# A table of steps for a router and eight experts: one small product one chunk later, one group behind another, two widenings moved into the last round

## The chip, the cores and the metric

The kernel runs on one core of one Trainium2 chip. The time is that of the device for one execution, in microseconds (us). The engines are TensorE (PE, with PEld for its loads of weights), VectorE (DVE), ScalarE (ACT), GpSimd (POOL) and SyncE (SP, which issues most DMAs). Each runs its own instructions in order and waits on semaphores for the others. TensorE has two clocks, 1.2 and 2.4 GHz; the profile tells the one granted as a share of the higher (0.50 or 1.00).

## The reference

```
x   = causal softmax attention(q, k, v)          # 2 x 12 heads x 448 x 64, gathered to 896 x 768
logits = x @ w_gate                              # 896 x 8
# greedy: in the order of falling logit, a token takes an expert that has fewer than 112 tokens
for e in range(8):
    h = maximum(x[assigned == e] @ w1[e], 0)     # 112 x 768 @ 768 x 1024
    y[assigned == e] = h @ w2[e]                 # 112 x 1024 @ 1024 x 768
yn  = y / sqrt(mean(y * y, -1) + 1e-6) * rms_g
out = (silu(yn @ w_g) * (yn @ w_val)) @ w_out    # 768 -> 1536 -> 768, all 896 rows
```

Everything is in 32-bit floats. Where a product is split, each operand is the sum of a rounded high part (hi) and the rest (lo), and three products stand for one: hi by hi, lo by hi, hi by lo.

## The kernel before

Attention comes first, head by head, then eight rounds, one for an expert each, then the rest of the feed-forward part. The rounds are written as strings of words, which a function emits one after the other; TensorE, VectorE, ScalarE and GpSimd carry out their instructions exactly in that written order, whereas SyncE's loads and the feed-forward part behind the rounds are put in order by a scheduler. Round 0 uses the string ITER0, rounds 1 to 5 ITER, round 6 ITER6 and round 7, which has no next expert, LASTR; END follows. A word is a letter, a chunk number, and an optional `'` or `+` for work that belongs to another round.

- `U0` to `U7`: eight chunks of the expert's first product (hp, line 626, six matmuls each, on the gathered and transposed rows xf and the raw weights). `A`, `H`: its relu (ScalarE, hh, line 634) and the low part of that (VectorE, hl, line 638).
- `Z0` to `Z7`: a chunk of the second weights is split, hi by a cast on ScalarE (line 574), lo on VectorE (line 575). `Z0+` belongs to the next round. `D0` to `D7`: the second product (y, line 651, six matmuls each).
- `N0` to `N2`: the norm of the previous expert's y (lines 660 to 666, result yn). `Y0`, `Y1`: its transposes (tp, line 587) and the split of them (xnh on ScalarE, xnl on VectorE, lines 598 and 599).
- `X0`, `X1`: transposes of the next expert's gathered rows (tp<-cs,xg) and the copies xf of them on ScalarE (line 596).
- The router of a later round: `M1` transposes the best logits m to rows mr (line 402) and copies them to ms on ScalarE; `G` (lines 411 to 415) compares, `P0` to `P6` count (pc, line 423), `Q0`, `Q1` rank and pick an expert, `O` makes a one-hot tile (VectorE, line 493), `F0'` multiplies it with token numbers (pi, line 501, seven small matmuls), `F1'` makes row numbers idx of that (VectorE, line 505) and issues the gather xg, `Q2'` names the expert, whose weights may then be loaded.
- `B0` to `B7` load half-rows of the feed-forward weights (SyncE, w, line 519), `C0` to `C7` widen them (a cast g on ScalarE, line 524, then five operations on VectorE, lines 528 to 532, about 2.45 us in all), `J` splits the widened halves (lines 536, 537), `I0` and `I1` make the table of output rows (pr, line 690, its two copies to ms, line 692; pt, line 696, idt on VectorE, line 697), `K` are the first gate products (line 548).

PSUM tiles of the router (mr, pc, ptot, pi, pr, pt) share the tag "r", which has two banks. `M1` asks for two of them, one for four transposes and one for three:

```
for t0, t1 in ((0, 4), (4, NT)):
    mr = bank("r", "mr")
    for t in range(t0, t1):
        nc.tensor.transpose(mr[:, (t - t0) * 128:(t - t0 + 1) * 128],
                            self.m[:, t:t + 1].to_broadcast([128, 128]), ident)
    nc.scalar.copy(self.ms[:, t0 * 128:t1 * 128], mr[:, :(t1 - t0) * 128])
...
with tc.manual_schedule(engines={ET.PE, ET.Activation, ET.DVE, ET.Pool}):
    emit(START0, -2)
    emit(START1, -1)
    for r in range(E):
        emit(ITER0 if r == 0 else LASTR if r == E - 1 else ITER6 if r == E - 2 else ITER, r)
    emit(END, E)
```

Of the kernel before, what the change touches and what calls it, by code (L numbers as in the profile page):

```python
# [24 lines left out]
F1 = 1024  # L25
# [10 lines left out]
START0 = 'M0 M1 G G'  # L36
START1 = "G1' G' P0' P1' G' P2' P3' P4' G' P5' G1' P6' Q0' Q1' M1 O' G F0' F1' G P0 P1 Q2' G G G P2 P3 G X0 P4 P5 G X1 P6 U0+ Q0 U1+ U2+ Q1 U3+ U4+ O"
ITER0 = "Y1 A0 M1 N2 U5 G F0' G U6 Q2' F1' U7 Y0 G G G D0 N1 P0 P1 A1 P2 D1 D2 D3 G P3 D4 G X0 D5 P4 P5 P6 N0 D6 Q0 X1 D7 Z0+"
ITER = "U0 Q1' O' U1 Z1 Z2 N0 N1 U2 F0' F1' U3 Q2' A0 M1 N2 Z3 U4 H0 Z4 U5 Y0 Y1 Z5 G U6 G Z6 U7 A1 G D0 G P0 H1 G P1 D1 G D2 P2 Z7 G P3 D3 D4 D5 P4 P5 D6 X0 P6 D7 X1 Q0 Z0+"
LASTR = "U0 B2 U1 Z2 Z3 N0 N1 N2 I0 B3 U2 Z4 B4 U3 A0 B5 U4 Y0 Z5 H0 Y1 B6 U5 I1 Z6 C2 U6 B7 U7 A1 D0 H1 Z7 J0 D1 J1 C3 D2 D3 J2 C4 D4 J3 C5 D5 D6 D7 K0"  # L40
ITER6 = "U0 Q1' O' U1 Z1 Z2 N0 N1 U2 F0' F1' U3 Q2' A0 N2 Z3 U4 H0 Z4 U5 Y0 Y1 Z5 U6 Z6 U7 A1 D0 B0 H1 Z7 D1 B1 D2 D3 Z0+ D4 C0 D5 X0 Z1+ D6 C1 X1 D7"
PRE = 2
END = "N0 N1 N2 K1 Y0 Y1 J4 S0 J5 C6 K2 J6 C7 K3 J7 K4 K5 K6 S1 K7"
QK = 'dd'
# [27 lines left out]
def tile_attn_moe_ffn(ctx, tc, qk, v, consts, wts, wgv, wout, rmsg, out):  # L72
# [626 lines left out]
    def emit(words, r0):  # L699
        for w in words.split():  # L700
            op, c, r = w[0], int(w[1:].rstrip("'+") or 0), r0 + w.count("+")
            if op in "MGPQ" or op in "OF":
                k = r + 2 - (w[-1] == "'")
                if 0 <= k < E:
                    getattr(rounds[k], op)(c)
            elif op == "K":
                half, which, part = c // 4, c // 2 % 2, c % 2
                gate_val(half, which, range(3 * part, 3 * part + 3))
            elif op == "S":
                sg0[c] = cv.tile([128, S], F32, tag="sg", name="sg", bufs=2)  # L710
                nc.scalar.activation(sg0[c], gv0[c, 0][:, :S], AF.Silu)
            elif op == "Z":
                if r < E:
                    split(r, 8 + c)
            elif op == "I":
                turn_ids(c)
            elif op == "B":
                raws64.append(load64(half64(wgv, c)))
            elif op == "C":
                wide.append(widen(raws64[c]))  # L720
            elif op == "J":
                if c % 2 == 0:
                    early.append(tiles64())
                hi, lo = early[c // 2]
                c0 = c % 2 * 384
                halves(wide[c], hi[:, c0:c0 + 384], lo[:, c0:c0 + 384])
            elif op == "X":
                if r + 1 < E:
                    if c == 0 and r >= 0:
                        exps.append(Expert(r + 1))  # L730
                    getattr(exps[r + 1], op)(c)
            elif op in "NY":
                if r > 0:
                    getattr(exps[r - 1], op)(c)
            else:
                getattr(exps[r], op)(c)

    ET = mybir.EngineType
# [6 lines that stand above are left out]
# [143 lines left out]
```

## Time and profile before

| | us |
|---|---|
| three runs | 615.65, 613.38, 615.59 (median 615.59) |
| the profiled execution, its own time | 616.78 |
| its span in the profile | 615.0 |
| mean granted clock of TensorE | 0.972 |
| TensorE busy | 578.8 |
| VectorE busy | 468.1 |
| ScalarE busy | 271.6 |

A median is that of separate runs; the profile shows one more execution, of which all the rows below are. Its span goes from its first to its last instruction. A busy time sums what an engine works, without what it waits, so a time won is one in which TensorE stands still or runs at the lower clock.

### The profile page before, as it was taken

Reading aid. Unit: us, or ns where it says so; the run is one execution under the profiler, and the core shown is the slowest. Engines: PE = TensorE matmul, PEld = TensorE weight load, DVE = VectorE, ACT = ScalarE, POOL = GpSimd, SP = SyncE. Lnnn points to the kernel's source line nnn. Section 1 sums busy time; section 2 is a strip of 40 time slices with the busy share of each in tenths; the row PEclk is TensorE's granted clock in tenths of the full one; section 3 lists DMA queues with packets and bytes.
Section 4 is the critical chain, followed back from the end, with each engine's and each line's share of the span. In section 5 each row is a group of like instructions: output and inputs, shape, how many; then the busy total and the mean of one; then the engine's idle time right before and its main releaser. Section 6 shows DMA issues by size and latency. Waiting matters only on the chain.

```text
span 615.0 us, 11157 instructions
## 1 busy us (share of the span) xinstructions
PE 578.8 (94%) x3926; PEld 541.4 (88%) x3926; DVE 468.1 (76%) x1246; ACT 271.6 (44%) x617; POOL 97.6 (16%) x102
## 2 busy tenths in 40 slices
PE   4899999858999999999979999999999999999996
PEld 3799999748699999999969899999999999999995
DVE  7699999695588888978757799999998992991410
ACT  4799998501252353444434343444333434331200
POOL 4688775140100000000000000000000000000210
PEclk9999999957999999999979999999999999999998
DMA  8988881109996968869796243445444550000211
GB/s 276 259 253 256 244 242 41 31 6 376 317 355 227 335 219 309 284 210 350 279 345 194 78 138 122 151 155 144 125 141 130 155 134 21 27 1 1 103 39 39
DMA packets 47976, 109.35 MB, mean 178 GB/s; under 512 B 15232, under 2 KB 17408, under 8 KB 47920
## 3 DMA queue, kind: packets, MB, share of 16 engines
q1 hardware_dynamic: 45280, 93.96, 46.7%
q0 software_dynamic: 2640, 14.68, 7.5%
q8 instruction: 31, 0.51, 0.3%
q14 instruction: 25, 0.20, 0.1%
HBM read 103.12 MB, written 5.51 MB: 177 GB/s over the span
## 4 chain that ended last, share of the span: by engine, by line
PE 72%; DVE 13%; DMA 7%; issue 3%; ACT 2%; SPq 1%; POOL 1%; POOLq 0%; DVEq 0%; ACTq 0%
PE o L795 14%; PE pv L774 13%; PE pg L774 13%; PE hp L626 6%; PE sp L174 4%; PE pt L203 4%; PE ot L233 4%; PE y L651 4%; PE pn L260 3%; DMA raw<-in_wts 3%; DVE lo L575 2%; DVE G L415 2%; DMA w<-in_wgv 2%; PE pg L548 2%; DMA cs<-in_consts 2%
## 5 line engine op out<-in xcount | busy, mean ns | idle before, releaser
L626 PE MATMUL hp<-xf,raw 128*128 128x112 f32 x768 | 96.1, 284 | 4.0 <-ACT xf L596 4.0
L626 PEld LDWEIGHTS hp<-xf,raw 128*128 128x128 f32 x768 | 92.9, 200 | 4.9 <-ACT xf L596 4.4
L575 DVE TENSOR_TENSOR lo<-raw,hi 128x768 fp32r<-128x768 f32 x56 | 52.7, 955 | 15.3 <-ACT hi L574 15.0
L802 POOL DMA_INDIRECT out<-ob,idt x7 | 6.8, 969 | 306.9 <-ACT ob L801 298.4
L536 ACT CAST hi<-t 128x384 fp32r<-128x384 f32 x58 | 29.5, 510 | 49.2 <-DVE t L532 49.0
L195 ACT ACTIVATE pe<-sm,nm 128x256 f32<-128x256 f32 (+3 forms) x84 | 48.7, 582 | 2.5 <-DVE nm L185 2.1
L774 PE MATMUL pv<-xnh,hi 128*128 128x448 f32 x132 | 48.6, 368 | 0.0
L774 PE MATMUL pv<-xnl,hi 128*128 128x448 f32 x132 | 48.6, 368 | 0.0
L774 PE MATMUL pv<-xnh,lo 128*128 128x448 f32 x132 | 48.6, 368 | 0.0
L774 PE MATMUL pg<-xnh,hi 128*128 128x448 f32 x132 | 48.6, 368 | 0.0
L774 PE MATMUL pg<-xnl,hi 128*128 128x448 f32 x132 | 48.6, 368 | 0.0
L774 PE MATMUL pg<-xnh,lo 128*128 128x448 f32 x132 | 48.6, 368 | 0.0
L203 PE MATMUL pt<-cs,pe 128*128 128x128 f32 x228 | 41.3, 288 | 3.8 <-DVE ptl L220 2.6
L185 DVE CUSTOM_DVE_ANT_0 sm<-sp,mask 128x384 f32<-128x384 f32 (+3 forms) x84 | 42.1, 514 | 3.2 <-PE sp L174 2.3
L574 ACT CAST hi<-raw 128x768 fp32r<-128x768 f32 x56 | 44.3, 840 | 0.3 <-DMA raw<-in_wts 0.3
L524 ACT ACTIVATE g<-w 128x384 f32<-128x384 f32 x72 | 39.6, 553 | 8.8 <-DMA w<-in_wgv 8.7
L220 DVE TENSOR_TENSOR ptl<-pt,pth 128x512 fp32r<-128x512 f32 (+3 forms) x84 | 41.4, 514 | 2.5 <-ACT pth L216 2.5
L216 ACT CAST pth<-pt 128x512 fp32r<-128x512 f32 (+3 forms) x84 | 37.1, 444 | 10.9 <-PE pt L203 9.0
L529 DVE SCALAR_TENSOR_TENSOR t<-g,t 128x384 uint32<-128x384 uint32 x72 | 39.3, 554 | 0.2
L531 DVE SCALAR_TENSOR_TENSOR g<-w,g 128x384 f32<-128x384 uint32 x72 | 39.2, 554 | 0.2
L174 PE MATMUL sp<-hi 128*128 128x384 f32 (+3 forms) x84 | 32.9, 401 | 6.8 <-DVE hi L160 5.4
L532 DVE TENSOR_TENSOR t<-t,g 128x384 f32<-128x384 f32 x72 | 38.8, 554 | 0.2
(163 smaller groups left out, 1367.3 us busy)
## 6 DMA issues: line engine op xcount, KB each, us to landing
raw<-in_wts SPq DMA_DIRECT2D x128, 384.0 KB, 5.9
w<-in_wgv SPq DMA_DIRECT2D x48, 384.0 KB, 3.7
w<-in_wout SPq DMA_DIRECT2D x24, 384.0 KB, 3.1
hi<-in_qk POOLq DMA_DIRECT2D x10, 896.0 KB, 5.8
qr<-in_qk SPq DMA_DIRECT2D x11, 448.0 KB, 4.4
vr<-in_v SPq DMA_DIRECT2D x12, 224.0 KB, 3.0
xs<-xl SPq DMA_DIRECT2D x12, 224.0 KB, 3.2
kr<-in_qk SPq DMA_DIRECT2D x10, 224.0 KB, 3.3
```

What stands on the lines that cost most here:

```text
L174: nc.tensor.matmul(sp[:, :w], x[:, t * 128:t * 128 + 128], kh[:, w0:w0 + w], start=st, stop=not st)
L185: nc.vector.tensor_tensor_reduce(out=sm[:, :w], in0=sp[:, :w], in1=mask[:, MOFF[t]:MOFF[t] + w], op0=ALU.add, op1=ALU.min, scale=-0.125, s ...
L195: nc.scalar.activation(pe[:, :w], sm[:, :w], AF.Exp, bias=nm[:, t:t + 1], scale=-1.0, accum_out=sums[:, t:t + 1])
L203: nc.tensor.transpose(pt[:, b * 128:b * 128 + 128], pe[:, b * 128:b * 128 + 128], ident)
L220: nc.vector.tensor_sub(*rest.pop((h, t)))
L524: nc.scalar.activation(g, raw[:, :, 1].bitcast(F32), AF.Copy, scale=2.0 ** -112)
L529: nc.vector.scalar_tensor_tensor(t, gu, 0x80000000, t, op0=ALU.bitwise_and, op1=ALU.bitwise_or)
L574: nc.scalar.copy(hi, raw)
L575: nc.vector.tensor_sub(lo, raw, hi.bitcast(F32))
L626: nc.tensor.matmul(o, w[:, dc * 128:dc * 128 + 128], self.x[:, dc, :], start=(dc == 0), stop=(dc == 5))
L774: nc.tensor.matmul(dst[:, :S], w[:, dc * 128:dc * 128 + 128], x[:, dc, c0:c0 + S], start=(dc == 0 and n == 0), stop=(dc == 5 and n == 2))
L795: nc.tensor.matmul(o[u][:, :SQ], x[:, fc % 6, :], w[:, u * SQ:u * SQ + SQ], start=(fc == 0 and n == 0), stop=(fc == NFC - 1 and n == 2))
```

## The change

Only three strings change. In rounds 1 to 6 the product F0' and the row numbers F1' come behind U3 in place of U2. In rounds 1 to 5 the count P3 comes behind D3 in place of ahead of it. In round 6 the widenings C0 and C1 are left out; in round 7 C0 stands behind I0 and C1 behind Y1. Their loads B0 and B1 stay in round 6.

```
-ITER = "U0 Q1' O' U1 Z1 Z2 N0 N1 U2 F0' F1' U3 Q2' A0 M1 N2 Z3 U4 H0 Z4 U5 Y0 Y1 Z5 G U6 G Z6 U7 A1 G D0 G P0 H1 G P1 D1 G D2 P2 Z7 G P3 D3 D4 D5 P4 P5 D6 X0 P6 D7 X1 Q0 Z0+"
-LASTR = "U0 B2 U1 Z2 Z3 N0 N1 N2 I0 B3 U2 Z4 B4 U3 A0 B5 U4 Y0 Z5 H0 Y1 B6 U5 I1 Z6 C2 U6 B7 U7 A1 D0 H1 Z7 J0 D1 J1 C3 D2 D3 J2 C4 D4 J3 C5 D5 D6 D7 K0"
-ITER6 = "U0 Q1' O' U1 Z1 Z2 N0 N1 U2 F0' F1' U3 Q2' A0 N2 Z3 U4 H0 Z4 U5 Y0 Y1 Z5 U6 Z6 U7 A1 D0 B0 H1 Z7 D1 B1 D2 D3 Z0+ D4 C0 D5 X0 Z1+ D6 C1 X1 D7"
+ITER = "U0 Q1' O' U1 Z1 Z2 N0 N1 U2 U3 F0' F1' Q2' A0 M1 N2 Z3 U4 H0 Z4 U5 Y0 Y1 Z5 G U6 G Z6 U7 A1 G D0 G P0 H1 G P1 D1 G D2 P2 Z7 G D3 P3 D4 D5 P4 P5 D6 X0 P6 D7 X1 Q0 Z0+"
+LASTR = "U0 B2 U1 Z2 Z3 N0 N1 N2 I0 C0 B3 U2 Z4 B4 U3 A0 B5 U4 Y0 Z5 H0 Y1 C1 B6 U5 I1 Z6 C2 U6 B7 U7 A1 D0 H1 Z7 J0 D1 J1 C3 D2 D3 J2 C4 D4 J3 C5 D5 D6 D7 K0"
+ITER6 = "U0 Q1' O' U1 Z1 Z2 N0 N1 U2 U3 F0' F1' Q2' A0 N2 Z3 U4 H0 Z4 U5 Y0 Y1 Z5 U6 Z6 U7 A1 D0 B0 H1 Z7 D1 B1 D2 D3 Z0+ D4 D5 X0 Z1+ D6 X1 D7"
```

On TensorE, in the middle of one of rounds 2 to 5, these are the rows of the kernel before with what each waits for (six more pairs like the two rows of line 501 are left out):

```order
L626 MATMUL hp<-xf,raw 128x112 x5
L501 LDWEIGHTS O [waits DVE_49]
L501 MATMUL pi<-ids,O 112x2 [waits PE_49]
...
L626 MATMUL hp<-xf,raw 128x112 [waits DMAHW5_49]
L626 MATMUL hp<-xf,raw 128x112 x5
L402 MATMUL mr<-cs,m 128x128 [waits PE_49]
L402 MATMUL mr<-cs,m 128x128 x3
L402 MATMUL mr<-cs,m 128x128 [waits DVE_49]
L402 MATMUL mr<-cs,m 128x128 x2
L626 MATMUL hp<-xf,raw 128x112 [waits DMAHW7_49]
```

And the same place on TensorE in the changed kernel:

```order
L626 MATMUL hp<-xf,raw 128x112 [waits DMAHW5_49]
L626 MATMUL hp<-xf,raw 128x112 x5
L501 LDWEIGHTS O [waits DVE_49]
L501 MATMUL pi<-ids,O 112x2 [waits PE_49]
...
L402 MATMUL mr<-cs,m 128x128 [waits PE_49]
L402 MATMUL mr<-cs,m 128x128 x3
L402 MATMUL mr<-cs,m 128x128 [waits Activation_49]
L402 MATMUL mr<-cs,m 128x128 x2
L626 MATMUL hp<-xf,raw 128x112 [waits DMAHW7_49]
```

The product pi stands one chunk of hp further down, right ahead of the transposes mr. The second group of mr, which waited for VectorE (idx, which frees the bank of pi), waits for ScalarE now: that is the first of the two copies ms, which frees the bank of the first group. In round 1 it waits for idx in both kernels.

On ScalarE, at the junction of rounds 6 and 7, the difference begins with the last relu of round 6 and goes on past the two copies of pr (- of the kernel before, + of the changed one):

```order
 L634 ACTIVATE hh<-hp 128x448
-L574 CAST hi<-raw 128x768 x2
-L524 ACTIVATE g_4472<-w_4427 128x384
-L574 CAST hi<-raw 128x768
-L524 ACTIVATE g_4507<-w_4442 128x384
-L596 COPY xf<-tp 128x448
...
+L574 CAST hi<-raw 128x768 x3
+L596 COPY xf<-tp 128x448
...
 L692 COPY ms<-pr 1x448 x2
+L524 ACTIVATE g_4554<-w_4427 128x384
```

The two casts g of C0 and C1 no longer stand ahead of the copies xf; the first comes behind the copies of pr, in round 7.

On VectorE, in the changed kernel, the five operations of C0 stand behind yn of round 6's expert, and those of C1 behind the split of the transposes of yn:

```order
L666 SCALAR_TENSOR_TENSOR yn<-y,s_4534,gb 112x768
L528 TENSOR_SCALAR t_4556<-g_4554 128x384
...
L532 TENSOR_TENSOR t_4556<-t_4556,g_4554 128x384
L575 TENSOR_TENSOR lo<-raw,hi 128x768 x2
L638 SCALAR_TENSOR_TENSOR hl<-hp,hh 128x448
L599 TENSOR_TENSOR xnl<-tp,xnh 128x4x112
L599 TENSOR_TENSOR xnl<-tp,xnh 128x2x112
L528 TENSOR_SCALAR t_4612<-g_4610 128x384
...
L532 TENSOR_TENSOR t_4612<-t_4612,g_4610 128x384
L697 CAST idt<-pt 128x7
```

Behind idt VectorE's rows are those of before, up to the next yn.

## Rows read from the trace of the kernel before

**Rows 1.** The page, part 1: busy us, share, instructions.

```profile
PE 578.8 (94%) x3926; PEld 541.4 (88%) x3926; DVE 468.1 (76%) x1246; ACT 271.6 (44%) x617; POOL 97.6 (16%) x102
```

**Rows 2.** TensorE's waits: us in total, times, longest.

```profile
PE pi L501 <- DVE O L493: 2.5, 4, 0.6
```

**Rows 3.** Windows around round 7: length, busy us (count) by engine, clock, DMA share, GB/s.

```profile
311.20:315.25 4.05, 0.01 (x1) 0.00 (x0) 2.27 (x5) 2.29 (x5) 0.00 (x0) 0.86 1.03 401
315.25:320.94 5.69, 5.69 (x26) 5.41 (x27) 5.44 (x11) 2.75 (x6) 0.00 (x0) 0.50 0.88 280
346.65:365.00 18.35, 18.35 (x91) 16.67 (x90) 15.55 (x37) 8.68 (x18) 0.00 (x0) 1.00 0.28 88
```

**Rows 4.** Timeline of TensorE, rounds 6 and 7: start, busy us, [idle before].

```profile
315.25 5.46 PE L626 MATMUL hp<-xf,raw 128*128 128x112 f32 x24 [4.05 <-ACT xf L596]
320.64 1.82 PE L690 MATMUL pr<-cs,idxf 112*1 112x112 f32 x16
...
345.86 0.79 PE L587 MATMUL tp<-cs,yn 112*128 112x112 f32 x6 [0.64 <-DVE yn L666]
```

**Rows 5.** Timeline of ScalarE, the same rounds.

```profile
312.26 0.54 ACT L524 ACTIVATE g<-w 128x384 f32<-128x384 f32 x1 [7.97 <-DMA w<-in_wgv]
...
314.68 0.77 ACT L596 COPY xf<-tp 128x448 f32<-128x448 f32 x2
...
322.93 0.83 ACT L574 CAST hi<-raw 128x768 fp32r<-128x768 f32 x1
```

**Rows 6.** Timeline of TensorE, round 6, first half of the first product.

```profile
290.40 4.17 PE L626 MATMUL hp<-xf,raw 128*128 128x112 f32 x36
294.41 0.48 PE L501 MATMUL pi<-ids,O 128*112 128x2 bf16 x7
294.75 4.25 PE L626 MATMUL hp<-xf,raw 128*128 128x112 f32 x36
```

**Rows 7.** Timeline of VectorE, rounds 6 and 7.

```profile
312.84 0.36 DVE L528 TENSOR_SCALAR t<-g 128x384 uint32<-128x384 uint32 x1 [7.42 <-ACT g L524]
...
315.29 0.95 DVE L575 TENSOR_TENSOR lo<-raw,hi 128x768 fp32r<-128x768 f32 x1
...
318.60 1.82 DVE L575 TENSOR_TENSOR lo<-raw,hi 128x768 fp32r<-128x768 f32 x2
...
327.53 0.62 DVE L638 SCALAR_TENSOR_TENSOR hl<-hp,hh 128x448 fp32r<-128x448 f32 x1
328.07 0.91 DVE L599 TENSOR_TENSOR xnl<-tp,xnh 128x448 fp32r<-128x448 f32 x2
330.27 0.17 DVE L697 CAST idt<-pt 128x7 uint32<-128x7 f32 x1 [1.29 <-PE pt L696]
...
344.78 1.02 DVE L666 SCALAR_TENSOR_TENSOR yn<-y,s,gb 112x768 f32<-112x768 f32 x1
```

**Rows 8.** Timeline of TensorE, round 4, first product and router.

```profile
266.13 4.18 PE L626 MATMUL hp<-xf,raw 128*128 128x112 f32 x36
270.95 0.52 PE L501 MATMUL pi<-ids,O 128*112 128x2 bf16 x7 [0.63 <-DVE O L493]
271.33 1.57 PE L626 MATMUL hp<-xf,raw 128*128 128x112 f32 x12
272.74 0.93 PE L402 MATMUL mr<-cs,m 128*128 128x128 f32 x7
273.50 2.83 PE L626 MATMUL hp<-xf,raw 128*128 128x112 f32 x24
```

**Rows 9.** Timeline of ScalarE: both copies of round 4, a single one of round 0.

```profile
200.00 0.58 ACT L404 COPY ms<-mr 128x512 f32<-128x512 f32 x1
...
273.38 0.96 ACT L404 COPY ms<-mr 128x512 f32<-128x512 f32 x2
```

**Rows 10.** Timeline of TensorE, round 4: P2 with P3, then P4 with P5.

```profile
283.33 0.64 PE L423 MATMUL pc<-oh,G 128*128 128x8 bf16 x14
...
287.04 0.51 PE L423 MATMUL pc<-oh,G 128*128 128x8 bf16 x14
```

## The prediction, made before the changed kernel was timed

> **What bounds the kernel now.** I read the page first: TensorE is busy for 578.8 of the 615.0 us span, VectorE for 468.1, ScalarE for 271.6 [rows 1]. So time is won where TensorE waits, or where it runs at the lower of its two clocks, and an engine beside it matters only where TensorE ends up waiting for it. The profiled execution took 616.78 us, 1.19 above the median of 615.59; I make the sum against 616.78 and subtract the same amount from both.
>
> The waits of TensorE, read next, show two that the change touches. One is the product that makes the row numbers: it waits four times, 0.6 us each, for VectorE's one-hot tile O, 2.5 in all [rows 2]. The other stands in the stretches [rows 3] and the timeline [rows 4]: at the junction of rounds 6 and 7 the first product (hp) waits 4.05 us for ScalarE's copy xf. In that stretch TensorE is empty; in the next 5.69 us it is busy throughout but the granted clock is 0.50, that is 1.2 instead of 2.4 GHz. ScalarE's timeline says why xf is late [rows 5]: it stood 7.97 us at the cast of the first feed-forward half (g, line 524), until that half's DMA had landed, and xf is three instructions behind it in its written order.
>
> **Part 1: C0 and C1 leave round 6.** Without the two casts ScalarE reaches xf as soon as its transposes are done. These stand ahead of the last two groups of products D6 and D7 in TensorE's order, so xf is ready when D7 ends and the 4.05 go. Successive groups overlap by about 0.16 in the rows (290.40 + 4.17 = 294.57, next at 294.41 [rows 6]), so hp of round 7 starts at 311.04, not 315.25. Its first 24 matmuls took 315.25 to 320.64 = 5.39 at the low clock [rows 4]; 36 of them took 4.01 at the full one [rows 6], so 24 take 2.67. The product pr of I0 then starts at 311.04 + 2.67 = 313.71, which is 6.93 earlier.
>
> That isn't the gain, because the widenings now stand in round 7, and VectorE does them there. Its way, in its new order:
> - ScalarE is through with both copies of pr at 322.93 [rows 5]; 6.93 earlier is 316.00, and C0's cast is next. VectorE began 0.58 after such a cast started (312.26 to 312.84 [rows 5, 7]): 316.58.
> - C0's five instructions take 2.45 (312.84 to 315.29): 319.03.
> - Two low parts of weights 1.82: 320.85. The low half hl and the two xnl, 327.53 to 328.98, 1.45: 322.30.
> - C1, 2.45: 324.75.
> - From idt to the end of yn the instructions are the same as before: 330.27 to 345.80, 15.53 [rows 7]. yn ends at 340.28.
>
> TensorE's transposes of yn (Y0) started at 345.86, right behind yn, and had been ready 0.64 earlier, at 345.22 [rows 4]. Now TensorE is ready at 345.22 - 6.93 = 338.29 and yn comes at 340.28, and the transposes 0.06 behind it as before: it waits 2.05 instead of 0.64, and the last expert's output is transposed 5.52 earlier. So 6.93 were won and 1.41 are given back at Y0. Behind Y0 TensorE has no gap (18.35 busy of 18.35 [rows 3]) and the orders are the same, so 5.52 reaches the end. Bounds: 6.93 + 0.64 = 7.6 if VectorE isn't late at all, and 0 if C0's cast starts 5.5 later than worked out. I take **5.5**, since each step is a row of the same instruction.
>
> **Part 2: the row-number product behind chunk 3 (rounds 1 to 6).** In rounds 2 to 5 it waits 0.63 for O [rows 8]; a further chunk of hp, 4.01 / 3 = 1.34, ahead of it covers that. From the first hp to the fifth chunk a round takes 266.13 to 273.50, 7.37 [rows 8]. Without the wait, four chunks are 5.35 and the product 0.34 (294.41 to 294.75 [rows 6]), so the transposes mr start at 5.69 instead of 6.61: up to 0.92 a round, 3.7 for four.
>
> But the order of the changed kernel shows a new wait. The second group of mr now waits for ScalarE, in place of VectorE: it gets the PSUM bank that the first group leaves when ScalarE has copied it, where before it got the bank of the row numbers, free by then. ScalarE's copy started 0.64 after mr (272.74 to 273.38 [rows 8, 9]), and a copy alone lasts 0.58 [rows 9]: 5.69 + 0.64 + 0.58 = 6.91, with 0.04 for the signal 6.95. Three transposes at 0.109 (the 7 took 0.76) end at 7.28. The next chunk starts 0.09 earlier than before, not 0.92. Four rounds: **0.36**. Bounds: 3.7 if the copy is no obstacle, and -0.8, 0.2 a round, if each wait costs more than its row would show (7.37 - 5.35 - 0.34 - 0.76 for mr leaves 0.92 lost, where the row shows a wait of 0.63; the new wait may lose such a 0.3 more, too). Rounds 1 and 6 have no such wait (0.34 from product to next chunk at 294.41): nothing. In these two the row numbers, and with them the gather, come one chunk, 1.3, later; the gathered rows are needed only at X0, behind D4 or D5 of the same round, and the rest of the first product and half of the second hide it.
>
> The Trainium skill (Perfetto Trace Analysis, Matmuls) says that independent matmul groups should rotate through different PSUM banks, so that one's evacuation overlaps the next one's matmuls; here two neighbouring groups now share one. By it this part wins little, as by the rows; by the diff alone it would win 3.7. No row of before shows the wait.
>
> **Part 3: P3 behind D3 (rounds 1 to 5).** The pair P2, P3 took 0.64, the pair P4, P5 0.51 [rows 10]; 0.13 is P3's wait for its G. Between the products of D3 and D4 that wait is covered, but there is one more switch between kinds of matmul. Bounds 0 and 0.13 a round; half, 0.07, five times: **0.35**.
>
> **Sum.** 5.52 + 0.36 + 0.35 = 6.23: 616.78 becomes 610.55, and the median 615.59 becomes 609.4. Half a per cent, 3.1 us, is about what a measurement of this kernel can tell from no change; this is twice that.
>
> **Rivals.**
> - **A, the router pays in full**: the copy is through sooner than I think, or the bank isn't the one waited for. 3.7 instead of 0.36: 606.0. For it: O's wait is plain in the rows. Against it: the new wait in the order. 0.15.
> - **B, the clock falls again at Y0.** After 4.05 idle TensorE ran 5.69 at half speed [rows 3], which at full speed would be 2.85; if 2.05 idle does the same the gain shrinks by 2.84, to 612.2. Before, 0.64 idle left the clock at 1.00 (346.65 on). The new 2.05 lies between the two, nearer the one that cost nothing. 0.15. [...]
> - **C, the widenings eat the gain**: something makes C0 late in round 7 (its half loaded behind others, or the copies of pr later), VectorE ends yn where it did, and TensorE waits for it. It decides from a C0 that starts near 322 instead of 316.6; 615. Against it: the half had landed by 312.26. 0.08.
> - **D, slower**: the new bank wait grows. If ScalarE reaches the first copy of mr late, since casts of weights that have not landed stand before it, TensorE stands at mr. Slower by 0.5% needs 6.23 + 3.1 lost over four rounds, 2.3 more in each, a wait of over 3 us. ScalarE is busy for 44% only [rows 1], and no cast is placed between the relu and that copy. 0.04.
>
> **Chances.** My forecast 0.58, A 0.15, B 0.15, C 0.08, D 0.04. The likeliest case has its own range of 608.0 to 610.6, from the bounds of parts 2 and 3 and a few tenths at Y0. The range that leaves out C, D and the edge of A is 605.6 to 612.4. Faster by over 0.5% is below 612.5: my case, A and two thirds of B, 0.83; within it the rest of B and C, 0.13; slower 0.04.
>
> **What would show it.** In the changed kernel's trace: no wait for xf at round 7, a clock of 1.00 through it, pr at about 313.7 less what the rounds before gained; a wait of about 2 us at the transposes of yn, and the clock behind it; no wait for O, but four of about 0.8 at mr for the copy ms. It would be wrong if a chunk of expert 7's weights landed late, since these chunks are asked for at the same places but used 7 us earlier, or if VectorE had idle time in the 15.53 from idt to yn that I count as work.

## The result and the profile after

| | before | after |
|---|---|---|
| median of four runs each, us | 615.62 (613.38 to 615.79) | 606.48 (605.23 to 609.21) |
| ratio, with its 95% interval | | 0.9866 (0.9824 to 0.9908) |
| profiled execution, us | 616.78 | 607.18 |
| span, us | 615.0 | 605.4 |
| mean granted clock | 0.972 | 0.979 |

The kernel got faster by 9.1 us, inside the range and in the direction forecast; the point forecast was 6.2, and the median of 606.48 lies below the 608.0 to 610.6 that was given for the likeliest case. The changed kernel was then timed a second time, beside another 23 runs of the kernel before on one chip: 607.69 against 613.18, ratio 0.9899 (0.9861 to 0.9936), 5.5 us. The two intervals, 5.7 to 10.8 us and 3.9 to 8.5 us, overlap. What do the profiles say of the difference? I cut each profiled execution into five stages by marks in TensorE's timeline: the first hp of rounds 1, 6 and 7, the last transposes of yn (Y0), the last gate or value matmul of line 774 (line 775 in kernels with e5's edit), and the end. All times are us; the labels of the other kernels are those of the experiments below.

| kernel | rounds 1 to 5 | round 6 | round 7 to Y0 | Y0 to last of line 774 | rest |
|---|---|---|---|---|---|
| before | 121.27 | 24.85 | 30.61 | 175.27 | 93.87 |
| after | 121.18 | 20.64 | 28.82 | 171.90 | 93.88 |
| e1_widen_only | 121.31 | 20.64 | 28.81 | 175.27 | 93.86 |
| e2_row_only | 121.35 | 25.55 | 30.60 | 171.90 | 93.88 |
| e3_p3_only | 121.09 | 25.36 | 30.88 | 175.27 | 93.87 |
| e4_after_again | 121.21 | 20.64 | 28.82 | 171.90 | 93.85 |
| e5_m_split | 117.53 | 20.64 | 28.82 | 171.90 | 93.86 |
| e6_c5_late | 121.21 | 20.64 | 26.99 | 171.84 | 93.86 |
| e7_both | 117.48 | 20.63 | 27.00 | 175.22 | 93.86 |
| e8_before_again | 121.27 | 25.12 | 30.14 | 175.27 | 93.86 |
| e9_both_again | 117.57 | 20.64 | 26.99 | 171.84 | 93.85 |
| e10_widen_again | 121.28 | 20.64 | 28.83 | 175.27 | 93.86 |
| e11_after_third | 121.22 | 20.64 | 28.83 | 175.27 | 93.87 |
| e12_split_no_widen | 117.54 | 25.94 | 30.09 | 171.90 | 93.88 |

Before against after: 0.09 in the rounds, 6.00 from round 6 to Y0, and 3.37 in the gate and value products, which no part of the change touches. The third and fourth columns are the change; the fifth takes one of two values in every kernel, within 0.06 us, and is the subject of several runs below. What stands ahead of round 1 isn't in the table. It took 169.13 us before and 168.99 after, and from 167.20 (e6) to 171.05 (e7) over the 14 profiles; the two profiles of e7's program alone are 2.51 apart in it.

**The junction.** TensorE's timeline of the changed kernel, rows 4 redone:

```profile
310.81 2.83 PE L626 MATMUL hp<-xf,raw 128*128 128x112 f32 x24
313.57 1.69 PE L690 MATMUL pr<-cs,idxf 112*1 112x112 f32 x16
...
339.62 0.80 PE L587 MATMUL tp<-cs,yn 112*128 112x112 f32 x6 [1.66 <-DVE yn L666]
```

The 4.05 in front of hp are gone, its first 24 matmuls end after 2.76 (5.39 before), and Y0 now waits 1.66 for yn (0.64 before). The windows of the changed kernel (columns as in rows 3) show the clock at 1.00 through hp, and again behind the wait at Y0:

```profile
311.00:313.57 2.57, 2.57 (x25) 2.46 (x25) 2.27 (x4) 1.20 (x3) 0.00 (x0) 1.00 1.03 402
...
340.00:360.00 20.00, 20.00 (x103) 18.56 (x102) 16.83 (x41) 8.85 (x18) 0.00 (x0) 1.00 0.27 85
```

ScalarE reaches xf as soon as its transposes are there (the releaser is TensorE, no longer a DMA behind a cast), and does C0's cast behind the copies of pr; its timeline, rows 5 redone:

```profile
308.71 0.78 ACT L596 COPY xf<-tp 128x448 f32<-128x448 f32 x2 [3.29 <-PE tp L587]
...
315.73 0.54 ACT L524 ACTIVATE g<-w 128x384 f32<-128x384 f32 x1
```

VectorE's timeline, rows 7 redone, is the chain that was summed:

```profile
316.30 0.36 DVE L528 TENSOR_SCALAR t<-g 128x384 uint32<-128x384 uint32 x1 [2.73 <-ACT g L524]
...
318.75 1.82 DVE L575 TENSOR_TENSOR lo<-raw,hi 128x768 fp32r<-128x768 f32 x2
320.49 0.62 DVE L638 SCALAR_TENSOR_TENSOR hl<-hp,hh 128x448 fp32r<-128x448 f32 x1
321.02 0.91 DVE L599 TENSOR_TENSOR xnl<-tp,xnh 128x448 fp32r<-128x448 f32 x2
321.85 0.35 DVE L528 TENSOR_SCALAR t<-g 128x384 uint32<-128x384 uint32 x1
...
324.30 0.16 DVE L697 CAST idt<-pt 128x7 uint32<-128x7 f32 x1
...
338.55 1.02 DVE L666 SCALAR_TENSOR_TENSOR yn<-y,s,gb 112x768 f32<-112x768 f32 x1
```

From C0's first operation on there is no idle mark up to yn, in the rows left out either: VectorE sets the time of Y0.

**The rounds.** TensorE's timeline of the changed kernel in round 4, rows 8 redone:

```profile
265.91 5.52 PE L626 MATMUL hp<-xf,raw 128*128 128x112 f32 x48
271.27 0.48 PE L501 MATMUL pi<-ids,O 128*112 128x2 bf16 x7
271.61 0.63 PE L402 MATMUL mr<-cs,m 128*128 128x128 f32 x4
272.91 0.54 PE L402 MATMUL mr<-cs,m 128*128 128x128 f32 x3 [0.68 <-ACT ms L404]
273.29 2.83 PE L626 MATMUL hp<-xf,raw 128*128 128x112 f32 x24
```

The wait for O has gone, and mr is cut in two by a wait for ScalarE's first copy, which is this row:

```profile
272.27 0.59 ACT L404 COPY ms<-mr 128x512 f32<-128x512 f32 x1 [0.26 <-PE mr L402]
```

The other bank of the tag wasn't free much earlier. VectorE reads the row numbers out of it in this row, behind two low parts of weights and a reciprocal in its order:

```profile
272.47 0.21 DVE L505 TENSOR_SCALAR idx<-pi 112x1 uint32<-112x1 f32 x1
```

It ends at 272.68, and the second group starts at 272.91. So in the bank of the row numbers the group would still have waited, by some 0.2 us less; that is an estimate from these two rows.

TensorE's waits over the whole changed kernel (columns as in rows 2):

```profile
PE mr L402 <- ACT ms L404: 2.7, 4, 0.7
...
PE tp L587 <- DVE yn L666: 1.7, 1, 1.7
```

Rows 2 had 2.5 us in four waits for O; there are 2.7 in four waits for ms now. From the first hp to the fifth chunk it takes 273.29 - 265.91 = 7.38, against 7.37 [rows 8].

### The profile page after: what moved, and what is told of

It reads as the page before. It is cut to its first block, busy times and chain, and to the rows that moved or that the text cites. A ratio compares the mean times of both kernels' runs of the same rounds, so it can differ in the third digit from the quotient of the medians.

```text
span 605.4 us, 11163 instructions
## 1 busy us (share of the span) xinstructions
PE 571.1 (94%) x3926; PEld 537.0 (89%) x3926; DVE 468.1 (77%) x1246; ACT 273.4 (45%) x617; POOL 98.4 (16%) x102
## 4 chain that ended last, share of the span: by engine, by line
PE 86%; DVE 5%; DMA 3%; ACT 2%; issue 2%; SPq 1%; POOL 1%; POOLq 0%; DVEq 0%; ACTq 0%
PE o L795 14%; PE pv L774 13%; PE pg L774 13%; PE hp L626 12%; PE y L651 10%; PE sp L174 4%; PE pt L203 4%; PE ot L233 4%; PE pn L260 3%; DMA cs<-in_consts 2%; PE pg L548 2%; PE tp L587 2%; PE pc L423 1%; PE mr L402 1%; DVE G L415 1%
## 5 line engine op out<-in xcount | busy, mean ns | idle before, releaser
L626 PE MATMUL hp<-xf,raw 128*128 128x112 f32 x768 | 91.9, 278 | 0.0
L626 PEld LDWEIGHTS hp<-xf,raw 128*128 128x128 f32 x768 | 89.6, 195 | 0.5 <-issue 0.2
```

What stands on the lines that cost most here:

```text
L626: nc.tensor.matmul(o, w[:, dc * 128:dc * 128 + 128], self.x[:, dc, :], start=(dc == 0), stop=(dc == 5))
```

## The experiments

Two questions were open: which part of the change gives what, and whether the 3.4 us in the gate and value products come from it. My theory: only part 1 pays, the new wait eats part 2, and the 3.4 belong to the single execution. The rival: they belong to the program.

**The parts one by one.** e1 takes part 1 alone, e2 part 2 alone, e3 part 3 alone, each as an edit of the kernel before:

```diff
-ITER6 = "... D3 Z0+ D4 C0 D5 X0 Z1+ D6 C1 X1 D7"
+ITER6 = "... D3 Z0+ D4 D5 X0 Z1+ D6 X1 D7"
-LASTR = "... N2 I0 B3 ... H0 Y1 B6 ..."
+LASTR = "... N2 I0 C0 B3 ... H0 Y1 C1 B6 ..."
```

```diff
-ITER = "... U2 F0' F1' U3 Q2' A0 ..."
+ITER = "... U2 U3 F0' F1' Q2' A0 ..."
-ITER6 = "... U2 F0' F1' U3 Q2' A0 ..."
+ITER6 = "... U2 U3 F0' F1' Q2' A0 ..."
```

```diff
-ITER = "... P2 Z7 G P3 D3 D4 ..."
+ITER = "... P2 Z7 G D3 P3 D4 ..."
```

e4 is the changed kernel once more, not altered.

> Only the two widenings are moved (part 1 alone). My theory: the wait for xf and the stretch at the lower clock go, yn ends late, so Y0 starts 5.5 to 6.1 us earlier than before and waits about 1.7 us; from there on nothing differs but the pace of the gate and value matmuls, which belongs to the single execution: 206.7 or 202.7 ns from one matmul to the next, 3.2 us over the 792. Median 606.5 to 610.5 us. Rival: the pace belongs to the program, and the moved widenings made it 202.7: then always 202.7 here, and a median of 606 to 607, all of the changed kernel's gain.

> Only the row-number product stands one chunk later (part 2 alone). My theory: no wait for the one-hot tile, four waits of about 0.7 us at the second group of mr for the first copy ms, so a round is as long as before within 0.05 us: median 615 to 616 us, or some 3 us less if the executions have the faster pace. Rival (the part pays): 2.5 to 3.7 us less before the feed-forward part begins.

> Only P3 stands behind D3 (part 3 alone). My theory: 0.03 to 0.07 us a round, 0.2 to 0.35 us in all, not to be seen in the median (615 to 616 us but for the pace). Rival: it moves other things, and the rounds get shorter by 1 us or more.

> The changed kernel, not altered. If the pace of the gate and value matmuls belongs to the single execution, its new profile may show 206.7 ns as well as 202.7, and the times spread over some 3 us or more; if it belongs to the program, the profile shows 202.7 again. Median 605.5 to 609 us.

| | median, us | ratio to the kernel before (613.18) |
|---|---|---|
| e1_widen_only | 607.18 | 0.9878 (0.9844 to 0.9912) |
| e2_row_only | 613.84 | 0.9998 (0.9974 to 1.0023) |
| e3_p3_only | 613.01 | 0.9990 (0.9963 to 1.0016) |
| e4_after_again | 607.69 | 0.9899 (0.9861 to 0.9936) |

Part 1 alone is the whole gain: its stages from round 6 to Y0 are 20.64 + 28.81, those of the changed kernel, against 24.85 + 30.61. Part 2 alone wins nothing: its trace has the same four waits of 0.68 us for ms, and its rounds are 0.08 us longer than before. Part 3 alone wins 0.18 us in its five rounds. The pace came out in a way that didn't settle it: e1 and e3 have the longer time of before in the fifth column, e2 and e4 the shorter one, as if it went with part 2, while e2's median says that part 2 gives nothing.

**The pace, by profiles of the same program.** Three of the kernels and one from below (e7, with the edits of e5 and e6) were run again, not altered. Each is a single run: e8 615.66, e9 601.24, e10 610.59 and e11 610.25 us.

> The kernel before, not altered, for a second profile. If the pace of the gate and value matmuls belongs to the single execution, it may be 202.7 ns here (206.7 in its first profile); if it belongs to the program, it is 206.7 again. All other marks as in the first profile within some tenths, but for the start.

> The kernel with both edits once more, not altered, for a second profile. If the pace of the gate and value matmuls belongs to the single execution, it may be 202.7 ns here (206.7 in its first profile) and the run then some 3 us shorter, 602 to 604 us; if it belongs to the program, it is 206.7 again and the run 605 to 607 us.

> The kernel with the widenings alone once more, not altered. By the single execution: 202.7 or 206.7 ns (206.7 in its first profile), and a run of 606 or of 609 us accordingly; by the program: 206.7 again.

> The changed kernel once more, not altered, after two profiles at 202.7 ns. By the single execution: 202.7 or 206.7, and a run of 607 or of 610 us; by the program: 202.7 again.

The value products by tile (duration in ns: least, median, most; then the first and the last start in us) of, first, the changed kernel in its first profile and in its third:

```profile
L774 PE MATMUL pv<-xnh,hi x132: 362/365/369, 351.2 to 511.1; 128*128 128x448 f32 x132
```

```profile
L774 PE MATMUL pv<-xnh,hi x132: 368/368/369, 351.1 to 514.2; 128*128 128x448 f32 x132
```

and of the kernel with both later edits, e7, in its first profile and, as e9, in its second:

```profile
L775 PE MATMUL pv<-xnh,hi x132: 368/368/368, 347.9 to 511.0; 128*128 128x448 f32 x132
```

```profile
L775 PE MATMUL pv<-xnh,hi x132: 362/365/370, 345.3 to 505.2; 128*128 128x448 f32 x132
```

The changed kernel takes 159.9 us from the first start to the last in one execution and 163.1 in another, both without a wait; e7 163.1 and 159.9. So the program doesn't fix the pace; the rival, as it was put, falls. The two runs of the changed kernel differ by little else: their other four stages agree within 0.04 us, the part ahead of round 1 is 0.34 shorter in the second, and the times are 607.18 and 610.25. The changed kernel showed the shorter time twice and the longer once, e7 each of them once, the kernel before and e1 the longer one twice; over the 14 profiles it stands 7 to 7. One thing these profiles leave open: all five of kernels without part 2 have the longer time, and seven of nine with it the shorter. The medians don't bear out that part 2 makes the shorter one likelier (e2, with it, 613.84 against 613.18; e1, without it, 607.18, and the changed kernel 607.69), but no run was made to settle it. Of the 9.60 us between the first two profiles, 3.37 were this, and the 0.14 ahead of round 1 is of the same sort, a difference between executions; 0.09 stands in the rounds and 6.00 from round 6 to Y0. Which pace the runs without a profile had isn't known.

**The new wait, and yn.** Two edits of the changed kernel. e5 makes two words of M1, so that the second group of mr comes one chunk of hp behind the first; e6 puts the last widening of round 7 behind yn of the last expert; e7 does both. The first fence is e5 (in START0, START1 and ITER0 the word M2 stands right behind M1), the second e6.

```diff
-            self.ms = rt.tile([128, N], F32, tag="ms", name="ms", bufs=1)
-            for t0, t1 in ((0, 4), (4, NT)):
+            if c == 1:
+                self.ms = rt.tile([128, N], F32, tag="ms", name="ms", bufs=1)
+            for t0, t1 in (((0, 4),), ((4, NT),))[c - 1]:
...
-ITER = "... A0 M1 N2 Z3 U4 H0 ..."
+ITER = "... A0 M1 N2 Z3 U4 M2 H0 ..."
```

```diff
-LASTR = "... J3 C5 D5 D6 D7 K0"
+LASTR = "... J3 D5 D6 D7 K0"
-END = "N0 N1 N2 K1 Y0 ..."
+END = "N0 N1 N2 C5 K1 Y0 ..."
```

> The changed kernel, with the two groups of mr as two words: the second group stands behind U4, so the first copy ms runs beside a chunk of hp. My theory: the four waits of 0.68 us for ms are what takes part 2's gain, so without them a round gets 0.65 to 0.9 us shorter, 2.6 to 3.6 us over four rounds, and the median falls to 603.5 to 605.5 us. Rival: the later second copy makes G and the counts P late, the wait goes there, and the time stays at 606 to 608 us.

> The changed kernel, with the last widening of round 7 (C5) behind yn of the last expert. My theory: yn is late at Y0 because VectorE does 2.45 us of widening more ahead of it, so the wait of 1.66 us for yn falls below 0.3, and Y0 starts 1.4 to 1.7 us earlier: median 1.5 us below the changed kernel. Rival: yn waits for something else (ScalarE's sum of squares, y itself), and Y0 stays where it is.

> The changed kernel with both edits, the second group of mr behind U4 and C5 behind yn. My theory: the two gains add, 4 to 5 us, median 602 to 604.5 us. Rival: only one of them is left, 605 us or more.

| | median, us | ratio to the kernel before (613.85) |
|---|---|---|
| e5_m_split | 604.32 | 0.9831 (0.9794 to 0.9869) |
| e6_c5_late | 604.85 | 0.9839 (0.9801 to 0.9876) |
| e7_both | 602.99 | 0.9798 (0.9758 to 0.9838) |

TensorE's timeline of e5 in round 4:

```profile
263.12 5.52 PE L627 MATMUL hp<-xf,raw 128*128 128x112 f32 x48
268.48 0.48 PE L502 MATMUL pi<-ids,O 128*112 128x2 bf16 x7
268.81 0.63 PE L403 MATMUL mr<-cs,m 128*128 128x128 f32 x4
269.28 1.49 PE L627 MATMUL hp<-xf,raw 128*128 128x112 f32 x12
270.61 0.49 PE L403 MATMUL mr<-cs,m 128*128 128x128 f32 x3
270.93 1.49 PE L627 MATMUL hp<-xf,raw 128*128 128x112 f32 x12
```

No idle mark is left, and rounds 1 to 5 take 117.53 instead of 121.18: 3.65 us, almost exactly the 3.7 that the diff alone promised. The wait didn't move to the counts, so the new wait was what ate part 2. It cost 0.91 a round where its row shows 0.68. Against the kernel before the rounds are 3.74 shorter, of which 0.18 is part 3's by e3. In e6 the same transposes of yn start without a wait,

```profile
336.04 0.74 PE L587 MATMUL tp<-cs,yn 112*128 112x112 f32 x6
```

and round 7 to Y0 is 26.99 instead of 28.82, 1.83 us, a little more than the wait shown. In e7 both columns have the low value, so the gains add in the stages, 5.5 us over the changed kernel; its median is the lowest of all kernels here, 2.0% below before by the ratio, though its interval overlaps those of e5 and e6. Its first profile (607.02) took 5.78 us longer than its second, e9 (601.24): the pace makes 3.38 and the part ahead of round 1 makes 2.51 of that, less 0.1 elsewhere.

**Is part 1 needed for what the rounds win?** e12 is e5 with the widenings where they were before.

```diff
-ITER6 = "... D3 Z0+ D4 D5 X0 Z1+ D6 X1 D7"
+ITER6 = "... D3 Z0+ D4 C0 D5 X0 Z1+ D6 C1 X1 D7"
-LASTR = "... N2 I0 C0 B3 ... H0 Y1 C1 B6 ..."
+LASTR = "... N2 I0 B3 ... H0 Y1 B6 ..."
```

> Parts 2 and 3 with the second group of mr behind U4, but the widenings where they were before (part 1 undone). My theory: rounds 2 to 5 win 3.6 us ahead of the junction, as in the kernel with part 1, but ScalarE still stands at the first widening until its half has landed, and the landing moves by much less; so the wait for xf grows by 2 to 3.5 us, and of the 3.6 at most 1.5 are left behind it. Median 0 to 1.5 us below the kernel before. Rival: the half's load is asked for earlier too and lands earlier by as much; then 3 to 3.6 us reach the end without part 1.

Median 609.53 against 613.08, ratio 0.9929 (0.9897 to 0.9962). My expectation was wrong, the rival right for most of it. ScalarE's timeline of e12 has the first widening (columns as in rows 5):

```profile
309.12 0.54 ACT L525 ACTIVATE g<-w 128x384 f32<-128x384 f32 x1 [9.06 <-DMA w<-in_wgv]
```

and TensorE's wait for xf is this row:

```profile
PE hp L627 <- ACT xf L597: 5.1, 1, 5.1
```

The rounds won 3.73. The cast began 3.14 earlier (312.26 in rows 5), but 0.50 of that lies ahead of round 1: counted from there, SyncE asked for the half 3.62 earlier (303.92 before, 299.80 in e12) and it landed 2.64 earlier. So most of the gain went on: round 6 lost 1.09 by a wait of 5.1 instead of 4.05, and round 7 to Y0 was 0.52 shorter; TensorE ran at the granted clock of 0.50 for 4.50 us of it (312.12 to 316.62), and for 5.69 before. The 0.57 that is left of the two is less than the spread of these two stages in the other four profiles with the widenings in round 6 (55.26 to 56.24 us). Here a load that is asked for from within the rounds moved with them.

## Why the prediction was right, step by step

**Part 1, 5.52 forecast, 6.00 measured.** The mechanism held at each link: hp of round 7 starts when D7 ends, at the full clock; C0's first operation was forecast for 316.58 and came at 316.30; C1 ended at about 324.30, where idt begins, for 324.75; Y0 came at 339.62 for 340.34. Each is early by 0.23 because round 7 began that much earlier (0.14 ahead of round 1, 0.09 in the rounds); this is no part of the 6.00. The 0.48 by which part 1 was forecast too small has three pieces. C0's first operation came 0.05 sooner behind the start of the round. Another 0.17 is overlap that I had left out: I took durations where starts lie closer (two low parts 1.74 from start to start, not 1.82; hl and xnl 1.36, not 1.45). The rest, 0.26, is in the last step: idt to the end of yn took 324.30 to 339.57, 15.27, where rows 7 gave 15.53. Most of it is at the low half hl and the low part of weights behind it, whose starts lie 0.73 apart before (333.70 and 334.43) and 0.53 after (327.68 and 328.21). That was the slack I had named as a danger, and it was on the good side. TensorE's wait at Y0 was forecast as 2.05 and is 1.66: yn came the 0.48 sooner, and TensorE itself was there 0.10 sooner. The kernel before has a spread of its own in these stages: by its second profile, e8, part 1 is 5.80.

**Part 2, 0.36 forecast, nothing measured** (0.08 lost in e2). The new wait stands where the order of the changed kernel put it, 0.68 us long, forecast about 0.8. The copy began 0.66 after mr and took 0.59 (0.64 and 0.58 forecast); from the restart of mr to the next hp there were 0.38 instead of 0.33, and the signal took 0.05. These tenths were the whole of the 0.09 a round. What was measured lies within the bounds given for this part, in their lower part. By the order of the program the second group waits for the copy that frees the first group's bank, 2.7 us in four rounds; with a chunk of hp between them, in e5, the waits are gone and 3.65 us with them. The rule of the Trainium skill (Perfetto Trace Analysis, Matmuls), that independent groups should rotate through different PSUM banks so that one's evacuation overlaps the next one's matmuls, fits the kernel before, where the second group got the other bank and the seven transposes of rows 8 show no wait. In the changed kernel the other bank would have saved only about 0.2 of the 0.68, by the row of idx above. So sharing a bank isn't the whole cause: neither bank was free when TensorE got there, at 272.23, and what helped was work in between.

**Part 3, 0.35 forecast, 0.18 measured** in e3: 0.04 a round, not 0.07. In round 4, from start to start, the counts P2 and P3 took 0.38 together in e3 and 0.50 before, and the products D3, D4 and D5 took 3.28 and 3.20 before. So of the 0.12 that was won the further switch between kinds of matmul took 0.08, more than the half I gave it.

**The rivals.** A, the router in full, would have come to 606.0, and the first median of 606.48 looks like it; the trace and e2 show that it isn't what happened. Its gain in the rounds is reached only with e5's edit. B, the clock falling at Y0: the wait was 1.66, and the clock behind it 1.00. C: C0 came on time. D: no sign. Had only the first four runs been there, the agreement of 606.5 with rival A would have been a trap: the right number for a wrong reason.

**The size.** The first three stages say 6.09 us for the change, the forecast was 6.23, the second timing 5.5 and the first 9.1. That 6.23 is so near to 6.09 is partly luck: part 1 was forecast 0.48 too small, and parts 2 and 3 together, 0.71 for the 0.09 of the rounds, 0.62 too large. What the forecast lacked beyond that was not a term of the change but the spread of the kernel itself between executions, 3.4 us by the pace and up to 2.5 ahead of round 1 for one and the same program, which I had taken as covered by half a per cent.

## What to carry to other kernels

A cast that waits for a DMA on an engine with a fixed order holds back everything behind it; when it is moved, follow both the engine that is relieved and the one that gets the work, because the gain ends where the second is late (here TensorE was ready for Y0 7.0 us sooner and waited there 1.0 longer, which left 6.0; moving one more widening behind yn, e6, won 1.8 more). When one wait is taken away, look in the new program at what the next instruction waits for, not only at what it did wait for: here a wait for a PSUM bank kept all of part 2's gain until something stood between the two groups. And when a profile of before and one of after are compared, cut them into stages: a difference in a stage that the change can't reach is to be run again before it is explained.

## What was not expected of the hardware

The 792 gate and value matmuls of line 774 run without a wait, at a granted clock of 1.00, either at 206.7 ns from start to start ((521.13 - 357.65) / 791, before) or at 202.7 ((511.53 - 351.22) / 791, after). At the longer pace single spacings are 205 to 208 ns; at the shorter one they vary between 198 and 208, with the same mean over each hundred matmuls. The pace holds from the first to the last within one execution and changes between executions of the same program, 3.2 us of the whole, or 3.4 with the first gate products ahead of them; the output products of line 795 behind them take the same time always (93.85 to 93.88 to the end). What sets it wasn't found. The stretch from round 6 to Y0 was 55.3 to 56.2 us in the five profiles that have the widenings in round 6. There round 6 is 20.80 us and the wait for xf, which hangs on a DMA's landing (4.05 to 5.14 us), and TensorE then ran for 4.50 to 6.28 us at a granted clock of 0.50. The stretch was 49.45 to 49.47 in the six that have the widenings where the changed kernel has them and C5 where it was; none of these shows the wait or the lower clock.
